# A two-layer recurrent-memory transformer and mixer on one core: weight blocks of one 128-row piece, a ring of their own for the mixer's weights, and one exponential per head group

## The chip, the core and the metric

The kernel runs on one core of a Trainium2 chip. Its engines work side by side and wait for each other through semaphores: TensorE (PE; its weight loads are listed apart as PEld), VectorE (DVE), ScalarE (ACT), GpSimd (POOL) and SyncE (SP). Here SP only issues loads of weights. The metric is the device time of one execution in microseconds (us).

## The reference, cut to what matters

The program is attention layer A, mixer B, A again, B again, each on the layer norm of a residual stream x of 2048 rows by 640 (bfloat16), with the same weights both times.

```python
# A: 64 segments of 32 rows, in order; mem (8 rows) goes from each segment to the next
for s in range(n_seg):
    h = concat([mem, x[32*s:32*s+32]])                     # 40 rows of 640
    q, k, v = h @ Wq, h @ Wk, h @ Wv                       # 32 heads of 192
    scores = where(mask, q @ k.T * scale, -1e9)
    o = (softmax(scores) @ v) @ Wo                         # back to 640
    mem, out[s] = o[:8], o[8:]
# B: token mixing by shifted column groups, then an MLP of 1536
h  = gelu(layernorm(x) @ w1)                               # 640 x 640
x1 = x + concat(four shifted column groups of h) @ w2      # 640 x 640
y  = x1 + gelu(layernorm(x1) @ w3) @ w4                    # 640 x 1536 x 640
```

The weights of A are 31.5 MB, more than the on-chip memory holds beside the activations, and every segment needs all of them.

## The kernel before

Both applications of A run interleaved as two lanes of one loop: step t handles segment t of the first layer and segment t-5 of the second, so that 64 + 5 = 69 steps do all of it. Steps 5 to 63 have both lanes (80 columns), the first five and the last five only one (40 columns). The mixer B runs in 35 chunks of 128 rows (64 of each lane), one for two steps, spread over the attention work of these steps.

A step has 8 groups of 4 heads. `proj` computes k, q (transposed, 6 tiles of 128 rows) and v of a group, and `attend` the scores (`pss`), mask and row minimum on DVE (L569), the exponential on ACT (L577, one instruction per head, each with the row's sum), the normalisation on DVE (L582, L583), the transposes (`pst`, L591), P times V (`pso`, L605) and the output projection into `psy` (L623), which adds up over the step. At the end of a step its first rows go to the next step's input (`hT`, L640): the next step can't begin before.

**Weights.** A's weights are cut into 64 units of 480 KB (half of a group's k, q, v or o; L387-L390). 37 of them stay on the chip (`N_RES`); 27 are loaded anew in each step into a ring of 5 buffers (`wst`, L423-L429). The mixer's weights come in up to 480 KB pieces of three 128-row blocks, through one buffer (`RING_B = 1`, `wstB`, L431-L462): 12 loads of this kind for a chunk, w1 in 2, w2 in 2 (the second in 5 transfers), w3 and w4 in 4 each. All these loads are issued by SP in one order; a load that waits for its buffer holds up those behind it.

**The order** of all instructions on all engines is written out ahead by a planner (`Plan.place`): each operation has an engine, an assumed duration and a due time; the planner places on each engine what can start first, the earlier due first among near ones, with an assumed transfer rate and latency for loads. The hardware then runs each engine's list in that order. A ring buffer or PSUM bank of a class ("P" 3, "S" 2, "B" 2, "y" 1) is handed out by the planner, too.

At the start, POOL copies w1 through on-chip memory into a reordered copy in device memory (`w1d`, L1013-L1026), which the chunks then read.

## Time and profile before

| what | us |
|---|---|
| median of the two runs shown (4161.6 to 4197.4) | 4179.5 |
| the profiled execution | 4201.7 |
| its span, first to last instruction | 4200.0 |
| PE busy / DVE busy / ACT busy in the span | 3679.9 / 2221.0 / 1960.1 |
| end of step 0 (first `hT` copy of L640) | 95.6 |
| end of step 4, start of the two-lane steps | 302.2 |
| end of step 62 (63rd `hT` copy) | 3775.9 |
| end of step 67 (68th `hT` copy) | 4040.8 |
| last attention matmul, then only mixer work | 4096 |

The table gives marks on the time axis; the stretch 302.2 to 3775.9 is 58 steps of both lanes, 59.9 us each. In the rows further down, "releaser" or "<-" names what ended an engine's idle time. The granted clock is TensorE's, as a share of 2.4 GHz (0.5 is 1.2 GHz). DMA share is the mean busy share of the 16 DMA engines; it can pass 1 where packets overlap.

### The profile page before, as it was taken

To read this page: it belongs to the slowest core of one execution; us is meant where nothing else is said; L and a number is where in the kernel's file an instruction comes from. 1 tells how busy PE (TensorE), PEld (TensorE's weight loads), DVE (VectorE), ACT (ScalarE), POOL (GpSimd) and SP (SyncE) were. 2 spreads that over 40 slices of the span, in tenths; PEclk is the share of its full clock that TensorE was granted. 3 is DMA by queue.
4 is the path that set the end of the run, shared out by engine and by line. 5 is a ranking of instruction groups with operands and counts; after the bars stand their busy time and mean duration, and the time that the engine had idled before them with its cause. 6 is when DMAs were issued, how large, how long until landed. Compare 5 with 4: busy or idle time off the path is not lost.

```text
span 4200.0 us, 162257 instructions
## 1 busy us (share of the span) xinstructions
PE 3679.9 (88%) x70351; PEld 3232.6 (77%) x70351; DVE 2221.0 (53%) x6403; ACT 1960.1 (47%) x7380; POOL 280.8 (7%) x489
## 2 busy tenths in 40 slices
PE   6998888889899898989898989888989888989993
PEld 4777877888888787878887888787878777877771
DVE  2455555555555555555555555555545555555452
ACT  2444444444454444544444544444544444445440
POOL 1000000000000000000000000000000000000000
PEclk7999999999999999999999999999999999999995
DMA  9998888888898888988888888888888888889992
GB/s 360 300 312 280 266 267 274 276 281 267 269 289 274 267 277 275 284 273 276 279 271 271 279 273 275 278 263 274 276 254 279 273 275 278 268 280 289 318 298 78
DMA packets 1365962, 1154.32 MB, mean 275 GB/s; under 512 B 44094, under 2 KB 1362380, under 8 KB 1365248
## 3 DMA queue, kind: packets, MB, share of 16 engines
q1 hardware_dynamic: 1357536, 1129.19, 86.0%
q0 software_dynamic: 7712, 14.76, 1.0%
q8 instruction: 552, 9.04, 0.8%
q14 instruction: 162, 1.33, 0.1%
...
## 4 chain that ended last, share of the span: by engine, by line
PE 67%; DMA 25%; issue 2%; SPq 2%; ACT 2%; DVE 1%; POOL 0%; ACTq 0%; POOLq 0%; DVEq 0%
DMA wstB<-in_B_w_dram 19%; PE psv L535 16%; PE psk L503 13%; PE psq L503 12%; PE psy L623 8%; DMA wstB<-w1d 4%; PE psh L928 3%; PE y L948 3%; PE pso L605 3%; PE pss L558 3%; PE pst L591 2%; PE psh L873 1%; PE hs L896 1%; SPq L460 1%; ACT Pm L577 1%
## 5 line engine op out<-in xcount | busy, mean ns | idle before, releaser
L577 ACT ACTIVATE Pm<-pss,sm 80x80 bf16<-80x80 f32 (+1 forms) x2208 | 673.3, 314 | 186.8 <-DVE sm L569 186.2
L540 ACT CAST V<-psv 80x384 bf16<-80x384 f32 (+1 forms) x1104 | 522.1, 474 | 507.4 <-PE psv L535 504.2
L535 PEld LDWEIGHTS <-hT 128*80 128x80 bf16 (+1 forms) x5520 | 586.4, 117 | 213.7 <-issue 15.8
L503 PEld LDWEIGHTS <-wst 128*128 128x128 bf16 x14490 | 611.3, 103 | 24.8 <-issue 5.9
L535 PE MATMUL psv<-wv,hT 128*80 128x384 bf16 (+1 forms) x3105 | 611.5, 332 | 2.3 <-DMA wv<-in_A_Wv_dram 2.1
L611 DVE CAST oT<-pso 128x480 bf16<-128x480 f32 (+1 forms) x552 | 342.3, 620 | 412.9 <-PE pso L605 411.5
L510 ACT CAST qT<-psq 128x480 bf16<-128x480 f32 (+1 forms) x552 | 292.1, 529 | 504.4 <-PE psq L503 493.9
L535 PE MATMUL psv<-wst,hT 128*80 128x384 bf16 (+1 forms) x2415 | 483.6, 332 | 0.7 <-DMA wst<-in_A_Wv_dram 0.4
L503 PE MATMUL psk<-hT,wk 128*128 128x80 bf16 (+1 forms) x9315 | 441.8, 205 | 17.6 <-ACT hT L640 13.0
L623 PE MATMUL psy<-oT,wo 128*128 128x80 bf16 (+1 forms) x10350 | 454.1, 200 | 2.2 <-DVE oT L611 1.5
L503 PE MATMUL psq<-hT,wq 128*128 128x80 bf16 (+1 forms) x9315 | 440.5, 203 | 5.8 <-DMA wq<-in_A_Wq_dram 5.7
L577 ACT ACTIVATION_READ_ACCUMULATOR Pm<-pss,sm 80x1 f32 (+1 forms) x2208 | 437.0, 198 | 0.0
L503 PEld LDWEIGHTS <-wk 128*128 128x128 bf16 x9315 | 396.8, 104 | 40.4 <-issue 22.2
L569 DVE CUSTOM_DVE_ANT_1 pss<-pss,mask 80x320 f32<-80x320 f32 x472 | 232.8, 493 | 358.5 <-PE pss L558 357.8
L623 PEld LDWEIGHTS <-wo 128*128 128x128 bf16 x10350 | 402.1, 100 | 14.7 <-issue 7.9
L596 ACT COPY PT<-pst 80x320 bf16<-80x320 bf16 (+1 forms) x552 | 221.5, 401 | 369.1 <-PE pst L591 365.3
L518 DVE CAST kT<-psk 128x320 bf16<-128x320 f32 (+1 forms) x552 | 256.3, 464 | 246.5 <-PE psk L503 243.6
L503 PEld LDWEIGHTS <-wq 128*128 128x128 bf16 x9315 | 379.0, 102 | 7.2 <-DMA wq<-in_A_Wq_dram 6.7
L503 PE MATMUL psk<-hT,wst 128*128 128x80 bf16 (+1 forms) x7245 | 357.1, 206 | 2.7 <-DMA wst<-in_A_Wk_dram 2.6
L503 PE MATMUL psq<-hT,wst 128*128 128x80 bf16 (+1 forms) x7245 | 342.4, 203 | 4.4 <-DMA wst<-in_A_Wq_dram 4.4
L524 DVE CAST kT<-psk 64x160 bf16<-64x160 f32 (+1 forms) x1104 | 336.7, 305 | 8.3
L623 PE MATMUL psy<-oT,wst 128*128 128x80 bf16 (+1 forms) x6210 | 284.0, 199 | 53.0 <-DVE oT L611 52.0
...
## 6 DMA issues: line engine op xcount, KB each, us to landing
wst<-in_A_Wk_dram SPq DMA_DIRECT2D x483, 480.0 KB, 5.3
wst<-in_A_Wq_dram SPq DMA_DIRECT2D x483, 480.0 KB, 5.5
wst<-in_A_Wv_dram SPq DMA_DIRECT2D x483, 480.0 KB, 5.2
wst<-in_A_Wo_dram SPq DMA_DIRECT2D x414, 480.0 KB, 5.5
wstB<-in_B_w_dram SPq DMA_DIRECT2D x315, 480.0 KB, 4.8
wstB<-w1d SPq DMA_DIRECT2D x35, 480.0 KB, 4.8
...
wstB<-in_B_w_dram SPq DMA_DIRECT2D x35, 160.0 KB, 3.8
```

Source lines behind the costliest of these rows:

```text
L503: nc.tensor.matmul(out=o[:, hf * GCH + cc, 0:N], lhsT=w[:, kc, cc * P:(cc + 1) * P], rhs=h[:, kc, c0:c0 + N], start=(kc == 0), stop=(kc == ...
L510: nc.scalar.copy(out=q[:, :, 0:N], in_=T(pq)[:, :, 0:N])
L518: nc.vector.tensor_copy(out=k4[:, :, 0::3, 0:N], in_=p4[:, :, 0::2, 0:N])
L524: nc.vector.tensor_copy(out=k4[r0:r1, :, j, 0:N], in_=p4[r0:r1, :, 1, 0:N])
L535: nc.tensor.matmul(out=o[0:N, :], lhsT=h[:, kc, c0:c0 + N], rhs=w[:, kc, :], start=(kc == 0), stop=(kc == KC - 1))
L540: nc.scalar.copy(out=v_runs(V_, hf)[0:N], in_=T(pv)[0:N, :].rearrange("n (a b) -> n a b", a=2))
L558: nc.tensor.matmul(out=o[0:N, i * N:(i + w_) * N].rearrange("p (a b) -> p a b", a=w_), lhsT=q[:, c, 0:N], rhs=k_[:, j:j + w_, 0:N], start= ...
L569: nc.vector.tensor_tensor_reduce(out=o, in0=o, in1=maskt[:].unsqueeze(1).to_broadcast([N, HG, N]), scale=-scale, scalar=3.0e38, op0=ALU.ad ...
L577: nc.scalar.activation(out=Pb[0:N, i, 0:N], in_=o[0:N, i * N:(i + 1) * N], func=ACT.Exp, bias=sm_[0:N, 0:1], scale=-1.0, accum_out=sm_[0:N ...
L596: nc.scalar.copy(out=Pt[0:N, :, 0:N], in_=T(pst)[0:N, :, 0:N])
L611: nc.vector.tensor_copy(out=o_[:, :, 0:N], in_=T(pso)[:, :, 0:N])
L623: nc.tensor.matmul(out=o[:, m, c0:c0 + N], lhsT=w[:, cc, m * P:(m + 1) * P], rhs=o_[:, hf * GCH + cc, 0:N], start=st, stop=True, skip_grou ...
```

## The change

Six things, all in the planner's input:

- A's weights are cut into 168 units of one 128-row block of a group: 192 KB for k, q, v (one contraction block, all 768 columns) and 160 KB for o. 102 of them (148,992 bytes a partition, before 142,080) stay; 66 are loaded in each step into a ring of 10 buffers of 192 KB. Over a step this is 12.39 MB instead of 13.27 MB. A projection unit adds its block into all 6 tiles of the group (6 matmuls), where before a unit finished 3 tiles (15 matmuls). The v unit adds into two PSUM banks at once.
- The mixer's weights have a ring of 5 buffers of 160 KB, one 128-row block per load: 34 loads a chunk instead of 12 in 16 transfers. w1, w3 and a rest of w2 are first copied at the start, by POOL's queue, into a reordered copy in device memory (`wbd`), 18 blocks of 160 KB.
- The exponential is one ACT instruction per group, in place in PSUM; the sums are a DVE reduction, and the normalisation reads PSUM.
- The two masked copies of k are two products with a 0/1 column (`halves`) over 128 rows.
- `after=last[0]` makes the projections of the plan follow each other, and o-buffers (`oT`) are 5 instead of 4, v-buffers 2 instead of 3. With them the output projections of the last 4 groups of a step, before 3, are due at its end.
- The planner's assumed rate, latency and look-ahead differ.

The diff, cut to its core:

```diff
-N_RES = 37
-RING_A = 5
-RING_B = 1
+RES_BYTES = 149000
+RING_A = 10
+RING_B = 5
 STEP = 48.0
 PSUM_POOLS = {"y": 1, "P": 3, "S": 2, "B": 2}
-OT_BUFS = 4
-V_BUFS = 3
+OT_BUFS = 5
+V_BUFS = 2
 LAT = 0.2
 PE_LAT = 0.25
-DMA_RATE = 350.0e3
+LOOK = 0.03
+DMA_RATE = 325.0e3
+DMA_LAT = 2.2
 
...
+        for kind in ("k", "q", "v"):
+            ORDER += [(kind, g, kc) for kc in range(KC)]
+        if g:
+            ORDER += [("o", g - 1, c) for c in range(GC)]
+    ORDER += [("o", NG - 1, c) for c in range(GC)]
+    total = sum(2 * w_len(u) for u in ORDER)
+    res_set = set()
+    acc = 0.0
+    share = RES_BYTES / total
+    got = 0
+    for u in ORDER:
+        n = 2 * w_len(u)
+        acc += share * n
+        if acc >= n / 2 and got + n <= RES_BYTES:
+            res_set.add(u)
+            acc -= n
+            got += n
...
         b = Slotted("ra", None)
-        b.make = lambda: wring.tile([P, HSZ], bf16, name="wst", tag=f"ra{b.slot}")
+        b.make = lambda: wring.tile([P, GW], bf16, name="wst", tag=f"ra{b.slot}")
 
         def fn(op):
-            nc.sync.dma_start(out=w_view(T(b), kind), in_=w_src(kind, g, hf))
-        add("SP", 0.06, due, fn, w=(b,), dma=P * HSZ * 2, queue="wa")
-        return b, lambda: w_view(T(b), kind)
-
-    def load_b(nm, a, e, due):
+            nc.sync.dma_start(out=T(b)[:, 0:n], in_=w_src(u))
+        add("SP", 0.06, due, fn, w=(b,), dma=P * n * 2, queue="wa")
...
+        b.make = lambda: wring.tile([P, Dm], bf16, name="wstB", tag=f"rb{b.slot}")
+        k = {"w1": n, "w3": KC + n, "w2": KC + FC}.get(nm)
+        rd = [] if nm == "w4" or (nm == "w2" and n < 4) else [B("wbd", k)]
+            nc.sync.dma_start(out=T(b)[:], in_=src)
...
+    def order_mixer_weights():
+
+        for n in range(KC):
+            def f(op, n=n):
+                o = wbd[n].rearrange("p (kc n) -> p kc n", kc=KC)
+                w1 = B_w1.rearrange("(kc p) n -> p kc n", p=P)
+                if n < 4:
+                    nc.gpsimd.dma_start(out=o, in_=w1[:, :, QD * n:QD * n + P])
+                    return
+                for gi in range(4):
+                    nc.gpsimd.dma_start(out=o[:, :, 32 * gi:32 * gi + 32], in_=w1[:, :, QD * gi + P:QD * gi + QD])
+            add("POOL", 0.9 if n < 4 else 4.0, 20 + n, f, w=(B("wbd", n),), dma=P * Dm * 2)
+
+        def f2(op):
+            for gi in range(4):
+                nc.gpsimd.dma_start(out=wbd[KC + FC][32 * gi:32 * gi + 32, :], in_=B_w2[QD * gi + P:QD * gi + QD, :])
+        add("POOL", 4.0, 26, f2, w=(B("wbd", KC + FC),), dma=P * Dm * 2)
+        for n in range(FC):
+            def f3(op, n=n):
+                o = wbd[KC + n].rearrange("p (kc n) -> p kc n", kc=KC)
+                nc.gpsimd.dma_start(out=o, in_=B_w3.rearrange("(kc p) n -> p kc n", p=P)[:, :, P * n:P * n + P])
+            add("POOL", 0.9, 30 + n, f3, w=(B("wbd", KC + n),), dma=P * Dm * 2)
 
...
             for kind, off in (("k", 0.0), ("q", 0.3 * sl)):
                 pq = ps("P", [P, GC, NS], f32, "ps" + kind)
-                for hf in range(2):
-                    due = s0 + off + hf * 0.1
-                    wb, wv = load_unit(t, (kind, g, hf), due)
-
-                    def fn(op, pq=pq, wv=wv, hf=hf):
+                now = []
+                for kc in range(KC):
+                    due = s0 + off + kc * 0.05
+                    wb, wv = load_unit(t, (kind, g, kc), due)
+
+                    def fn(op, pq=pq, wv=wv, kc=kc):
                         w, o = wv(), T(pq)
-                        for cc in range(GCH):
-                            for kc in range(KC):
-                                nc.tensor.matmul(out=o[:, hf * GCH + cc, 0:N], lhsT=w[:, kc, cc * P:(cc + 1) * P],
-                                                 rhs=h[:, kc, c0:c0 + N], start=(kc == 0), stop=(kc == KC - 1))
-                    add("PE", mm_us(N, k=GCH * KC), due, fn, r=(wb, *hk), a=(pq,))
+                        for c in range(GC):
+                            nc.tensor.matmul(out=o[:, c, 0:N], lhsT=w[:, c * P:(c + 1) * P], rhs=h[:, kc, c0:c0 + N],
+                                             start=pq.begin(), stop=True, skip_group_check=True)
+                    now.append(add("PE", mm_us(N, k=GC), due, fn, r=(wb, *hk), a=(pq,), after=last[0]))
+                last[0] = now
...
-                    for part, (r0, r1, j) in enumerate(((0, 64, 1), (64, P, 2))):
-                        def fk2(op, pq=pq, k_=k_, r0=r0, r1=r1, j=j):
-                            p4 = T(pq)[:].rearrange("p (h c) n -> p h c n", h=2)
-                            k4 = k_[:].rearrange("p (h c) n -> p h c n", h=2)
-                            nc.vector.tensor_copy(out=k4[r0:r1, :, j, 0:N], in_=p4[r0:r1, :, 1, 0:N])
-                        add("DVE", dve_us(2 * N), s0 + off, fk2, r=(pq,), w=(B("kT", G % 2, 1 + part),))
+
+                    def fk2(op, pq=pq, k_=k_):
+                        p4 = T(pq)[:].rearrange("p (h c) n -> p h c n", h=2)
+                        k4 = k_[:].rearrange("p (h c) n -> p h c n", h=2)
+                        for hf in range(2):
+                            nc.vector.tensor_tensor(out=k4[:, hf, 1:3, 0:N],
+                                                    in0=p4[:, hf, 1:2, 0:N].to_broadcast([P, 2, N]),
+                                                    in1=halves[:].unsqueeze(2).to_broadcast([P, 2, N]), op=ALU.mult)
+                    add("DVE", 2 * dve_us(2 * N), s0 + off, fk2, r=(pq,), w=(B("kT", G % 2, 1),))
             V_ = Vt[G % V_BUFS]
+            pv = [ps("P", [NS, GWH], f32, "psv") for _ in range(2)]
+            now = []
+            for kc in range(KC):
+                due = s0 + 0.6 * sl + kc * 0.05
+                wb, wv = load_unit(t, ("v", g, kc), due)
+
+                def fv(op, wv=wv, kc=kc):
+                    w = wv()
+                    for hf in range(2):
+                        nc.tensor.matmul(out=T(pv[hf])[0:N, :], lhsT=h[:, kc, c0:c0 + N],
+                                         rhs=w[:, GWH * hf:GWH * (hf + 1)], start=pv[hf].begin(), stop=True,
+                                         skip_group_check=True)
+                now.append(add("PE", mm_us(GWH, k=2), due, fv, r=(wb, *hk), a=tuple(pv), after=last[0]))
+            last[0] = now
             for hf in range(2):
...
-                o = T(pss)
-                for i in range(HG):
-                    nc.scalar.activation(out=Pb[0:N, i, 0:N], in_=o[0:N, i * N:(i + 1) * N], func=ACT.Exp,
-                                         bias=sm_[0:N, 0:1], scale=-1.0, accum_out=sm_[0:N, 4 + i:5 + i])
-            add("ACT", 4 * 0.31, hi - 4, f2, r=(pss, smk), w=(Pk, B("sm4", G % 4)))
+                o = T(pss)[0:N, 0:HG * N]
+                nc.scalar.activation(out=o, in_=o, func=ACT.Exp, bias=sm_[0:N, 0:1], scale=-1.0)
+            add("ACT", act_us(HG * N) + 0.09, hi - 4, f2, r=(smk,), w=(pss,))
 
             def f3(op):
+                o = T(pss)[0:N, 0:HG * N].rearrange("p (a b) -> p a b", a=HG)
+                nc.vector.reduce_sum(out=sm_[0:N, 4:4 + HG], in_=o, axis=AX.X)
                 nc.vector.reciprocal(out=sm_[0:N, 8:8 + HG], in_=sm_[0:N, 4:4 + HG])
-                nc.vector.tensor_tensor(out=Pb[0:N, :, 0:N], in0=Pb[0:N, :, 0:N],
+                nc.vector.tensor_tensor(out=Pb[0:N, :, 0:N], in0=o,
                                         in1=sm_[0:N, 8:8 + HG].unsqueeze(2).to_broadcast([N, HG, N]), op=ALU.mult)
-            add("DVE", 0.17 + 0.5, hi - 4, f3, r=(B("sm4", G % 4),), w=(Pk,))
+            add("DVE", 0.17 + 2 * dve_us(HG * N), hi - 4, f3, r=(pss,), w=(Pk, smk))
...
-            for hf in range(2):
+            for c in range(GC):
                 due = base + STEP - 1 + 0.02 * g if g >= NG - OT_BUFS + 1 else s0 + 2.0 * sl
-                wb, wv = load_unit(t, ("o", g, hf), s0 + (1.9 if g < NG - 1 else 1.2) * sl + 0.1 * hf)
-
-                def f8(op, wv=wv, hf=hf):
+                wb, wv = load_unit(t, ("o", g, c), s0 + (1.9 if g < NG - 1 else 1.2) * sl + 0.03 * c)
+
+                def f8(op, wv=wv, c=c):
                     w, o = wv(), T(psy)
-                    for cc in range(GCH):
-                        for m in range(KC):
-                            st = first_wo[0]
-                            first_wo[0] = False
-                            nc.tensor.matmul(out=o[:, m, c0:c0 + N], lhsT=w[:, cc, m * P:(m + 1) * P],
-                                             rhs=o_[:, hf * GCH + cc, 0:N], start=st, stop=True, skip_group_check=True)
-                add("PE", mm_us(N, k=GCH * KC), due, f8, r=(wb, B("oT", G % OT_BUFS)), a=(psy,))
+                    for m in range(KC):
+                        nc.tensor.matmul(out=o[:, m, c0:c0 + N], lhsT=w[:, m * P:(m + 1) * P], rhs=o_[:, c, 0:N],
+                                         start=psy.begin(), stop=True, skip_group_check=True)
+                add("PE", mm_us(N, k=KC), due, f8, r=(wb, B("oT", G % OT_BUFS)), a=(psy,))
...
         for i, (a, e) in enumerate(((0, 3), (3, KC))):
-            due = D(0.2 + 0.1 * i)
-            wb, wv = load_b("w1", a, e, due)
             pz = ps("B", [P, 3, XB], f32, "psh")
-
-            def fw(op, a=a, e=e, wv=wv, pz=pz):
-                w, o = wv(), T(pz)
-                for n in range(a, e):
+            for n in range(a, e):
+                due = D(0.15 + 0.04 * n)
+                wb, wv = load_b("w1", n, due)
+
+                def fw(op, n=n, a=a, wv=wv, pz=pz):
+                    w, o = wv(), T(pz)
                     for kc in range(KC):
-                        nc.tensor.matmul(out=o[:, n - a, :], lhsT=w[:, kc, (n - a) * P:(n - a + 1) * P],
+                        nc.tensor.matmul(out=o[:, n - a, :], lhsT=w[:, kc * P:(kc + 1) * P],
                                          rhs=vT[:, kc, 4:XB + 4], start=(kc == 0), stop=(kc == KC - 1))
-            add("PE", mm_us(128, k=KC * (e - a)), due, fw, r=(wb, vTk, B("vTl")), w=(pz,))
+                add("PE", mm_us(128, k=KC), due, fw, r=(wb, vTk, B("vTl")), a=(pz,))
...
-        for kc in range(KC):
-            def f6(op, kc=kc):
-                nc.gpsimd.dma_start(out=xo[:], in_=B_w1[kc * P:(kc + 1) * P, :])
-            add("POOL", 0.9, kc, f6, w=(B("xo"),), dma=P * Dm * 2)
...
+        order_mixer_weights()
```

Three places show how this moves instructions; the rows are of the lists in which the engines run them.

SP, in the middle of the run where a chunk's w4 is loaded (`wstB` from in_B_w_dram); in brackets the semaphores that the load waits for: PE is the release of its buffer, a DMAHW number the landing of an earlier load. Before:

```order
L427 DMA wst<-in_A_Wk_dram 128x5x384 [waits DMAHW6_49,PE_49]
L453 DMA wstB<-in_B_w_dram 128x3x640 [waits DMAHW7_49,PE_49]
L427 DMA wst<-in_A_Wq_dram 128x5x384 [waits DMAHW0_49,PE_49]
L427 DMA wst<-in_A_Wv_dram 128x5x384 [waits DMAHW1_49,PE_49]
L453 DMA wstB<-in_B_w_dram 128x3x640 [waits DMAHW5_49,PE_49]
L427 DMA wst<-in_A_Wo_dram 128x3x640 [waits DMAHW2_49,PE_49]
```

and with the change:

```order
L444 DMA wst<-in_A_Wk_dram 128x768 [waits DMAHW7_49,PE_49]
L444 DMA wst<-in_A_Wk_dram 128x768 [waits DMAHW0_49,PE_49]
L444 DMA wst<-in_A_Wq_dram 128x768 [waits DMAHW1_49,PE_49]
L462 DMA wstB<-in_B_w_dram 128x640 [waits DMAHW2_49,PE_49]
L462 DMA wstB<-in_B_w_dram 128x640 [waits DMAHW3_49,PE_49]
L462 DMA wstB<-in_B_w_dram 128x640 [waits DMAHW4_49,PE_49]
L444 DMA wst<-in_A_Wq_dram 128x768 [waits DMAHW5_49,PE_49]
L462 DMA wstB<-in_B_w_dram 128x640 [waits DMAHW6_49,PE_49]
```

Before, each `wstB` load reuses the one buffer of the load before it, so it stands behind PE's last matmul on that buffer; now the buffer that it reuses is that of five loads before. The DMAHW numbers run from 0 to 7 and begin again: with the change each load waits for the one issued eight loads earlier to land, so that at most eight are under way. In all there are 5846 weight loads on SP, before 2460 transfers.

POOL, at the start. Before, behind the memsets:

```order
L756 DMA xres<-in_A_x_dram 62x640
L761 DMA lnx<-in_A_x_dram 2x640
L767 DMA lnx<-in_A_x_dram 64x640
L862 COPY hTB<-hTB 128x5x8
L1015 DMA xo<-in_B_w_dram 128x640
L677 TENSOR_TENSOR st_146<-st_146,neghalf 128x2
```

and with the change:

```order
L473 DMA wbd<-in_B_w_dram 640x1x128 x4
L476 DMA wbd<-in_B_w_dram 640x1x32 x4
L707 TENSOR_TENSOR st_149<-st_149,neghalf 128x2
L481 DMA wbd<-in_B_w_dram 16x1280 x4
L486 DMA wbd<-in_B_w_dram 640x1x128 x12
L786 DMA xres<-in_A_x_dram 62x640
```

The `st` operation is a part of the first layer norm, which the first projection needs; eight transfers of w1 stand ahead of it now. The first `wstB` load from `wbd` stands 29th on SP's list and waits for the first of these copies.

DVE, one head group with both lanes. Before:

```order
L518 CAST kT_115<-psk 128x2x2x80
L524 CAST kT_115<-psk 64x2x80 x2
L569 ISA pss,sm_130<-pss,mask_78 80x320
L569 ISA sm_130 80x1
L611 CAST oT_125<-pso 128x480
L582 RECIPROCAL sm_130<-sm_130 80x4
L583 TENSOR_TENSOR Pm_120<-Pm_120,sm_130 80x320
```

and with the change:

```order
L545 CAST kT_115<-psk 128x2x2x80
L552 TENSOR_TENSOR kT_115<-psk,halves 128x160 x2
L644 CAST oT_123<-pso 128x480
L602 ISA pss,sm_130<-pss,mask_78 80x320
L602 ISA sm_130 80x1
L614 TENSOR_REDUCE sm_130<-pss 80x4
L615 RECIPROCAL sm_130<-sm_130 80x4
L616 TENSOR_TENSOR Pm_119<-pss,sm_130 80x320
```

One instruction more for DVE in each group (the sums), and the exponentials that ACT does between the mask and the reciprocal are one instead of four. PE's list has as many matmuls and weight loads as before (140,704 rows in both); only their order differs.

## Rows read from the trace of the kernel before

**Rows 1.** Windows (stretch and length; busy us and count per engine; granted clock, DMA share, GB/s).

```profile
0.00:95.60 95.60, 61.54 (x954) 41.58 (x955) 20.11 (x80) 23.75 (x104) 16.95 (x46) 0.72 1.05 364
...
302.20:3775.90 3473.70, 3108.40 (x59073) 2792.75 (x59073) 1918.31 (x5364) 1675.84 (x6205) 225.04 (x374) 0.95 0.88 274
...
3775.90:4040.80 264.90, 239.99 (x5062) 193.77 (x5063) 130.87 (x444) 126.16 (x524) 17.18 (x30) 0.97 0.96 307
...
4096.00:4200.00 104.00, 30.72 (x184) 18.84 (x180) 21.09 (x50) 8.88 (x18) 4.14 (x7) 0.52 0.27 79
```

**Rows 2.** Line L640 from 0 to 3780 us: end-of-step copies, first and last start.

```profile
L640 ACT CAST hT<-psy x63: 192/225/226, 95.6 to 3775.9; 128x80 bf16<-128x80 f32 x58, 128x40 bf16<-128x40 f32 x5
```

**Rows 3.** Waits of PE, 302.2 to 3775.9 us (us in total, times, longest).

```profile
PE y L948 <- DMA wstB<-in_B_w_dram: 87.7, 55, 3.3
PE psh L928 <- DMA wstB<-in_B_w_dram: 66.7, 30, 3.3
PE hs L896 <- DMA wstB<-in_B_w_dram: 56.2, 57, 2.1
PE psy L623 <- DVE oT L611: 46.9, 58, 0.9
PE psh L873 <- DMA wstB<-w1d: 44.6, 29, 2.5
PE pso L605 <- ACT PT L596: 39.3, 58, 0.8
PE pst L591 <- DVE Pm L583: 14.2, 29, 1.0
```

**Rows 4.** Chain of waits, 2078 to 2103 us: start, length, what, matmuls.

```profile
2078.99 0.84 PE psh L928 x15
2079.82 1.07 PE psq L503 x30
...
2081.71 0.15 PE pst L591 x4
2081.87 0.29 PE pss L558 x6
2082.16 0.81 PE psv L535 x5
2082.97 0.29 PE pso L605 x8
...
2086.28 5.95 DMA wstB<-in_B_w_dram
2092.28 1.78 PE psh L928 x15
2094.05 2.00 PE psk L503 x30
...
2101.94 0.83 PE y L948 x6
```

**Rows 5.** Waits of PE in the tail, 4096 to 4200 us.

```profile
PE y L948 <- DMA wstB<-in_B_w_dram: 27.5, 8, 3.7
PE psh L928 <- DMA wstB<-in_B_w_dram: 14.3, 4, 3.8
```

**Rows 6.** Page, part 6: loads, count, size, median us from issue to landing.

```profile
wst<-in_A_Wk_dram SPq DMA_DIRECT2D x483, 480.0 KB, 5.3
...
wstB<-in_B_w_dram SPq DMA_DIRECT2D x35, 160.0 KB, 3.8
```

**Rows 7.** The same in the tail, 4100 to 4200 us, one load at a time.

```profile
wstB<-in_B_w_dram SPq DMA_DIRECT2D x13, 480.0 KB, 3.4
```

**Rows 8.** Timeline of SP, 2030 to 2100 us: start, length of the issue.

```profile
2094.09 0.37 SPq L453 DMA_DIRECT2D wstB<-in_B_w_dram  x1
```

**Rows 9.** Groups of instructions by shape (busy us, mean ns, idle before).

```profile
L577 ACT ACTIVATE Pm<-pss,sm 80x80 bf16<-80x80 f32 x1888 | 584.8, 319 | 144.4 <-DVE sm L569 144.4
...
L569 DVE CUSTOM_DVE_ANT_1 pss<-pss,mask 80x320 f32<-80x320 f32 x472 | 232.8, 493 | 358.5 <-PE pss L558 357.8 <-issue 0.5
```

More of the change, by code (lines that the diff above doesn't have):

```diff
@@ L76, in add @@
         op.i = len(self.ops)
-        preds = set()
+        preds = set(after)
         slots = []
@@ L471, in lanes @@
         return r
+    last = [()]
     def HX(t):
@@ L844, in chunk @@
         psl2 = ps("B", [P, KC, 96], bf16, "psvl")
-        transposes(psl2, vx, 96, D(0.11), (vxk,))
+        transposes(psl2, lnx, 96, D(0.11), (B("lnx", "l"), B("lnx", "x")))
+        if c + 1 < NCH:
+            chunk_loads(c + 1)
         def fe(op):
@@ L885, in chunk, with fw @@
         hs = [ps("B", [XB, HC], f32, "hs") for _ in range(2)]
-        for i, (a, e) in enumerate(((0, 3), (3, 5))):
-            due = D(0.4 + 0.1 * i)
-            wb, wv = load_b("w2", a, e, due)
-            def fw(op, a=a, e=e, wv=wv):
+        for n in range(5):
+            due = D(0.4 + 0.04 * n)
+            wb, wv = load_b("w2", n, due)
+            def fw(op, n=n, wv=wv):
                 w = wv()
-                for n in range(a, e):
-                    off = W2OFF[n] if n < 4 else 0
-                    lhsT = hTB[:, n, off:off + TOK, :].rearrange("p w l -> p (w l)")
-                    for k in range(2):
-                        nc.tensor.matmul(out=T(hs[k])[:], lhsT=lhsT, rhs=w[:, n - a, HC * k:HC * (k + 1)],
-                                         start=(n == 0), stop=(n == 4))
-            add("PE", mm_us(HC, k=2 * (e - a)), due, fw, r=(wb, B("hTB", 0), B("hTB", 1)), a=tuple(hs))
+                off = W2OFF[n] if n < 4 else 0
+                lhsT = hTB[:, n, off:off + TOK, :].rearrange("p w l -> p (w l)")
+                for k in range(2):
+                    nc.tensor.matmul(out=T(hs[k])[:], lhsT=lhsT, rhs=w[:, HC * k:HC * (k + 1)],
+                                     start=hs[k].begin(), stop=True, skip_group_check=True)
+            add("PE", mm_us(HC, k=2), due, fw, r=(wb, B("hTB", 0), B("hTB", 1)), a=tuple(hs))
         for k in range(2):
```

169 lines of the change are left out of this document (63 added, 106 removed).

## The prediction

> **What bounds the kernel now.** I read the windows first, to see where PE is busy and at which clock; then PE's waits, to see what its idle time ends on; then the chain of waits, for the length of PE's pieces of work; then the loads. The 58 two-lane steps run from 302.2 to 3775.9 us [rows 1, 2], so one takes 3473.7/58 = 59.9 us. PE is busy 3108.4/58 = 53.6 us of it and idle 6.3. Of the idle time the four waits for `wstB` make (87.7 + 66.7 + 56.2 + 44.6)/58 = 255.2/58 = 4.4 us [rows 3]; nearly all of the rest is the end of a step, where the last group's scores go through DVE and ACT and PE has nothing else (46.9 + 39.3 + 14.2 = 100.4, 1.7 a step). A's own ring shows next to no wait.
>
> How much work does PE have? From the chain [rows 4], at the full clock: 30 matmuls of k, q or o take 1.07 us, 5 of v 0.81, the scores and P times V of a group 0.29 each, the transposes 0.15. A step has 24 times 30 of the first kind (25.7), 16 times 5 of v (13.0) and 8 groups of the rest (5.8): 44.5 us. A chunk has 85 matmuls like `psh` (0.84 for 15), 34 like `y` (0.83 for 6) and some 30 transposes at the `psh` rate: 4.8 + 4.7 + 1.7 = 11.2, half of it in each step. So 50.1 us of work in a step that takes 59.9. The 3.5 us between 50.1 and the 53.6 busy are partly TensorE's clock: 0.95 granted [rows 1] is a tenth of the time at 1.2 instead of 2.4 GHz, 6.0 us a step. One such place is in the chain: behind a `wstB` wait of 5.95 us, 15 `psh` take 1.78 instead of 0.84 and 30 `psk` 2.00 instead of 1.07, that is 1.9 us lost beside the wait [rows 4].
>
> So the bound in the steady part is PE's work, plus the one buffer of the mixer's ring: its next load can't be issued before PE's last matmul on the block before, and a load needs 3.4 us even alone [rows 7].
>
> **The change, part by part**, against the profiled execution (4201.7 us; the median of the runs shown is 0.5% less).
>
> *The mixer's ring of 5.* The load that PE needs next is issued four blocks ahead. A chunk has 34 blocks over two steps, one in 3.2 us on average, so four blocks are some 12 us, and 160 KB land in 3.8 us beside other loads [rows 6]. The 4.4 us a step go: -255 us. Ends: -255 and, if a fifth stays where blocks stand close together, -204.
>
> *The clock.* With the long waits gone, I expect the full clock in the steps. At most half of 6.0 us can come back, 3.0 a step; at least nothing, if the rest of the 3.5 is something else. I take 2.0, since the one stall in the chain alone lost 1.9 us: -116 us (0 to -174).
>
> *The other ten steps.* In the last one-lane steps PE is idle (264.9 - 240.0)/5 = 5.0 us each [rows 1], 3.1 more than a two-lane step has beside its ring waits (6.3 - 4.4 = 1.9). For ten such steps: -31 us (0 to -31).
>
> *The tail*, mixer alone, 104 us with PE busy for 30.7 [rows 1]. 12 waits for w4 and w3 blocks make 27.5 + 14.3 = 41.8 us [rows 5]. With loads ahead these go, and some waits for the GELU take their place: -35 (-20 to -42).
>
> *The start.* Step 0 needs all of A's weights and moves 364 GB/s [rows 1], so its length is set by loads. Added are 18 blocks of 160 KB, read and written: 5.9 MB, 16 us at that rate: +16. They are small pieces and w1 stands ahead of the first layer norm on POOL and of the 29th load on SP; eight transfers one behind the other at 3.8 us would be 30 us (0 to +30).
>
> *Traffic.* 12.39 + 2.79 MB a step instead of 13.27 + 2.79. The 284 GB/s that a step of 59.9 - 6.4 = 53.5 us would need is under the 307 of the one-lane steps [rows 1]. No gain is taken, the cover being PE's 50 us; without it a step's loads take 15.18 MB at 364 GB/s, 42 us. All this holds if small transfers move as fast: 480 KB ones gave 364 GB/s in step 0 with several under way [rows 1]. The Trainium skill (DMA: Bandwidth & Descriptors, Bandwidth) speaks against cutting them: it asks for transfers of 1 MiB or more for three quarters of the peak. By it the result would be that of rival 2, 4540, and by the rows it is 3760; the step 0 row shows that the rule doesn't bind at 480 KB, and no row shows 192 KB.
>
> *SP.* 66 + 17 = 83 issues a step at 0.37 us [rows 8] are 31 us of in-order work; 0.65 us each would make SP the bound.
>
> *Attention.* Four exponentials of 319 ns become one over 320 columns, at something like the 493 ns of the mask pass over the same data; the sum is another such pass on DVE [rows 9]. The end-of-step chain shortens by 1.28 - 0.49 and grows by 0.49: about 0.3 us less. DVE goes from 33.1 to some 37 us of a step: it stays off the path. v now takes both its PSUM banks at once, and the third belongs to q, so k must be out of its bank before v begins; q's 1.07 us and pieces between cover that in most groups. I take 0; ends -17 (0.3 a step) and +58 (1 us a step).
>
> *Finer projection units and more deferred o work.* As many matmuls, and a unit of 5 or 6 costs PE what a third of 15 does: `psy` already adds round-robin into its five tiles at 1.07 for 30. 0; if the extra o group fills half of the 1.7 us at a step's end, -50.
>
> Sum: 4201.7 - 255 - 116 - 31 - 35 + 16 = 3781; on the scale of the median, 0.5% less, 3760 us. All good ends together give 4201.7 - 255 - 174 - 31 - 42 - 17 - 50 = 3633, or 3613; all bad ones 4201.7 - 204 - 20 + 30 + 58 = 4066, or 4044. Half of the bad side is likely enough: 3620 to 3930 is the forecast's own range.
>
> **The rivals.**
>
> 1. *Eight loads in flight.* SP's list makes each load wait for the one eight earlier. Eight of 480 KB were plenty; now 83 loads a step, eight at a time, need 10.4 times the landing time. At 3.8 us [rows 6] that is 39 us and hidden. If a small load landed as late as a 480 KB one, 5.3 us, it would be 55.0 us: 58 x 4.9 = 284 saved instead of 371, 3868, or 3850. Against it: 160 KB landed in 3.8 in the same traffic.
>
> 2. *The same, on the slow side.* The landing time passes 5.8 us (59.9/10.4), from where a step is longer than now. At 6.2, that is 5.3 and half of the 1.9 by which load raises it over the 3.4 of a lone one [rows 6, 7], a step takes 64.5: 58 x 4.6 = +267, in the ten others some 11 us each, with tail and start 4560, or 4540. For it: more than twice as many transfers, with their completions, for the same bytes. Against it: rows 6. The rule above is of this kind; its chance is this rival's.
>
> 3. *The stall re-forms.* SP's list is in order, and a `wst` load that waits for PE holds the `wstB` loads behind it. If PE's list has mixer blocks just behind their loads, the 4.4 us stay, and with them the clock's loss; only the tail gains: 4201.7 - 35 + 16 = 4183, or 4160, no change. If half of both stays, it is 3997, or 3975.
>
> 4. *All bad ends of the terms together*: 4044, still faster.
>
> **How the numbers follow.** Forecast 0.73; better than 3620 0.07; between 3930 and 4096 (rival 3 with half, rival 4, rival 1 with landing somewhat over 5.3) 0.12; no change (rival 3 in full) 0.04; slower (rival 2) 0.04. Rival 1 at 3850 lies within the forecast's range, with 0.08 of its 0.73. A change of 2% is what a measurement of this kernel can tell, 4096 and 4263 us. Faster by over 2%: 0.73 + 0.07 + 0.12 = 0.92. The range of 8 in 10 is 3600 to 3940.
>
> **What would show it.** In the profile after: waits of PE for `wstB` under 1 us a step; granted clock 0.98 or more between the first and last steps; two-lane steps of 53 to 54 us with PE busy for 50 to 52; a tail of some 65 us; landing of `wst` near 4 us and PE's waits for it still near nothing; ACT busy down by a third or more, DVE up by a tenth. The forecast is wrong if PE waits for `wst` in mid-step (rival 1 or 2), if `wstB` waits stay (rival 3), or if the gaps at a step's end grow by more than 1 us.

## The result, and the profile after

The changed kernel takes **3825.1 us** (median; 3813.2 to 3836.9) against 4179.5: ratio **0.9152**, 95% interval 0.8944 to 0.936, so 8.5% faster. A second measurement of it, beside other kernels, gave 3814.2 us and 0.916 [0.9125, 0.9196]. Forecast were 3760 us, in a range from 3600 to 3940: the kernel got faster as forecast, and the time lies in the range, 1.7% above the forecast. The profiled execution took 3813.2 us; it is compared with the 4201.7 us of the one before.

The windows of the changed kernel, with the columns of [rows 1] (stretch and length; busy us of PE, PE's weight loads, DVE, ACT, POOL; granted clock, DMA share, GB/s): step 0, the four one-lane steps behind it, the 58 two-lane steps, steps 63 to 67 (63 still has both lanes, the others one), and the last step with the tail.

```profile
0.00:111.80 111.80, 74.50 (x954) 46.82 (x955) 21.41 (x90) 17.25 (x48) 25.79 (x50) 0.66 0.99 328
111.80:311.80 200.00, 188.12 (x4045) 144.64 (x4044) 105.96 (x389) 73.97 (x201) 12.09 (x21) 0.97 0.93 296
311.80:3445.40 3133.60, 2992.11 (x59067) 2668.23 (x59068) 2079.75 (x5825) 1276.72 (x2954) 207.57 (x374) 1.00 0.91 287
3445.40:3703.90 258.50, 243.59 (x5057) 191.39 (x5055) 140.95 (x485) 93.35 (x245) 16.36 (x30) 0.98 0.94 299
3703.90:3811.50 107.60, 76.63 (x1232) 55.52 (x1231) 54.55 (x168) 28.69 (x71) 9.44 (x18) 0.80 0.66 202
```

The bounds of the steps come from the end-of-step copies, the line that answers [rows 2]; it moved from L640 to L670.

```profile
L670 ACT CAST hT<-psy x68: 174/226/227, 111.8 to 3703.9; 128x80 bf16<-128x80 f32 x58, 128x40 bf16<-128x40 f32 x10
```

A two-lane step went from 59.9 to 3133.6/58 = 54.03 us. PE's busy time in these steps fell from 3108.4 [rows 1] to 2992.1 us for the same number of matmuls, at a granted clock of 1.00 instead of 0.95; its idle time fell from 365.3 to 141.5 us. What the idle time ends on, in the same stretch (us in total, times, longest), beside [rows 3]:

```profile
PE psv L566 <- ACT qT L537: 26.4, 86, 0.5
PE pso L638 <- ACT PT L629: 22.9, 57, 0.5
PE psy L653 <- DMA wst<-in_A_Wo_dram: 22.9, 30, 1.9
PE psy L653 <- DVE oT L644: 21.7, 29, 0.8
PE psk L529 <- DMA wst<-in_A_Wk_dram: 11.7, 25, 1.3
PE psq L529 <- DMA wst<-in_A_Wq_dram: 9.7, 20, 1.6
...
PE psv L566 <- DVE kT L552: 8.9, 28, 0.3
PE psv L566 <- DMA wst<-in_A_Wv_dram: 1.9, 5, 0.5
PE pst L624 <- DVE Pm L616: 0.8, 2, 0.6
...
PE y L975 <- DMA wstB<-in_B_w_dram: 0.5, 2, 0.3
PE hs L925 <- DMA wstB<-wbd: 0.4, 1, 0.4
```

Three things are to be seen. The four waits for `wstB`, 255.2 us before, are 0.9. The waits at a step's end (on `oT`, `PT`, `Pm`) fell from 100.4 to 45.4. And two kinds are new: A's streamed units (`wst`) cost 22.9 + 11.7 + 9.7 + 1.9 = 46.2 us, and v's banks, held by q (`qT`) and k (`kT`), 35.3 us.

The waits of the tail, from 3755 us on, beside [rows 5]: weights make 1.5 us, and VectorE's part of the GELU (`h2T`, `hTB`) now stands where they were.

```profile
PE y L975 <- DVE h2T L747: 4.2, 3, 2.5
PE psh L957 <- DVE h2T L747: 3.1, 2, 2.2
PE hs L925 <- DVE hTB L747: 2.9, 2, 1.8
PE y L975 <- DMA wstB<-in_B_w_dram: 1.5, 4, 0.7
```

The loads, as in [rows 6] (count, size, median us from issue to landing): a unit of 192 KB lands in 4.2 us, where 480 KB took 5.3.

```profile
wst<-in_A_Wk_dram SPq DMA_DIRECT2D x1104, 192.0 KB, 4.2
```

In step 0, where the loads set the time, the stretch from 30 to 90 us moved 377 GB/s before and 327 after (the first row is of the kernel before):

```profile
30.00:90.00 60.00, 43.11 (x635) 28.64 (x636) 11.25 (x46) 15.11 (x70) 3.42 (x7) 0.61 1.08 377
30.00:90.00 60.00, 45.70 (x572) 28.24 (x571) 9.87 (x40) 8.23 (x22) 0.00 (x0) 0.56 0.99 327
```

The exp and the sum, as in [rows 9] (busy us, mean ns of one, idle before): one exp of 494 ns stands for four of 319, and the sum takes VectorE 485 ns.

```profile
L609 ACT ACTIVATE pss<-pss,sm 80x320 f32<-80x320 f32 x472 | 233.4, 494 | 424.3 <-DVE sm L602 424.1
...
L614 DVE TENSOR_REDUCE sm<-pss 80x4 f32<-80x320 f32 x472 | 229.1, 485 | 188.2 <-ACT pss L609 186.5
```

### The profile page after: what moved, and what is told of

Its sections match the earlier page's. It is cut to its first block, busy times and chain, and to the rows that moved or that the text cites. A ratio compares the mean times of both kernels' runs of the same rounds, so it can differ in the third digit from the quotient of the medians.

```text
span 3811.5 us, 164549 instructions
## 1 busy us (share of the span) xinstructions
PE 3574.9 (94%) x70351; PEld 3106.6 (82%) x70351; DVE 2402.6 (63%) x6957; ACT 1490.0 (39%) x3516; POOL 271.2 (7%) x493
## 4 chain that ended last, share of the span: by engine, by line
PE 74%; DMA 18%; DVE 3%; ACT 2%; issue 1%; POOL 0%; SPq 0%; POOLq 0%; DVEq 0%; ACTq 0%
PE psv L566 20%; PE psy L653 13%; PE psk L529 12%; PE psq L529 12%; DMA wst<-in_A_Wk_dram 6%; DMA wst<-in_A_Wq_dram 5%; DMA wst<-in_A_Wo_dram 4%; PE pso L638 4%; PE pss L591 3%; PE y L975 3%; PE psh L957 2%; PE pst L624 2%; DMA wst<-in_A_Wv_dram 2%; ACT qT L537 1%; PE psh L903 1%
## 5 line engine op out<-in xcount | busy, mean ns | idle before, releaser
L566 PE MATMUL psv<-wv,hT 128*80 128x384 bf16 (+1 forms) x3312 | 799.1, 331 | 38.4 <-ACT qT L537 26.8
L529 PEld LDWEIGHTS <-wst 128*128 128x128 bf16 x13248 | 609.2, 100 | 76.2 <-DMA wst<-in_A_Wk_dram 32.7
L653 PE MATMUL psy<-oT,wo 128*128 128x80 bf16 (+1 forms) x10350 | 590.0, 199 | 30.5 <-DVE oT L644 25.5
L529 PE MATMUL psq<-hT,wq 128*128 128x80 bf16 (+1 forms) x9936 | 569.9, 199 | 6.0 <-DMA wq<-in_A_Wq_dram 4.7
L529 PE MATMUL psk<-hT,wk 128*128 128x80 bf16 (+1 forms) x9936 | 535.3, 199 | 15.9 <-ACT hT L670 11.9
L653 PEld LDWEIGHTS <-wo 128*128 128x128 bf16 x10350 | 466.8, 99 | 69.5 <-issue 45.4
L609 ACT ACTIVATE pss<-pss,sm 80x320 f32<-80x320 f32 (+1 forms) x552 | 261.7, 474 | 516.7 <-DVE sm L602 516.1
L653 PE MATMUL psy<-oT,wst 128*128 128x80 bf16 (+1 forms) x6210 | 417.1, 199 | 28.7 <-DMA wst<-in_A_Wo_dram 27.5
L529 PE MATMUL psq<-hT,wst 128*128 128x80 bf16 (+1 forms) x6624 | 412.4, 199 | 16.5 <-DMA wst<-in_A_Wq_dram 14.1
L614 DVE TENSOR_REDUCE sm<-pss 80x4 f32<-80x320 f32 (+1 forms) x552 | 254.3, 461 | 210.8 <-ACT pss L609 207.9
L653 PEld LDWEIGHTS <-wst 128*128 128x128 bf16 x6210 | 296.4, 99 | 44.5 <-DMA wst<-in_A_Wo_dram 34.7
```

The source lines that it names most:

```text
L529: nc.tensor.matmul(out=o[:, c, 0:N], lhsT=w[:, c * P:(c + 1) * P], rhs=h[:, kc, c0:c0 + N], start=pq.begin(), stop=True, skip_group_check= ...
L566: nc.tensor.matmul(out=T(pv[hf])[0:N, :], lhsT=h[:, kc, c0:c0 + N], rhs=w[:, GWH * hf:GWH * (hf + 1)], start=pv[hf].begin(), stop=True, sk ...
L609: nc.scalar.activation(out=o, in_=o, func=ACT.Exp, bias=sm_[0:N, 0:1], scale=-1.0)
L614: nc.vector.reduce_sum(out=sm_[0:N, 4:4 + HG], in_=o, axis=AX.X)
L653: nc.tensor.matmul(out=o[:, m, c0:c0 + N], lhsT=w[:, m * P:(m + 1) * P], rhs=o_[:, c, 0:N], start=psy.begin(), stop=True, skip_group_check ...
```

## The experiments

The theory was that the number of mixer loads that may be ahead of PE, and the clock that comes back with the stall, are the whole gain; the rivals were that other parts (finer units, less traffic, the single exp, the planner's constants) carry some of it. Each ratio is to the kernel before, measured on the same chip. One thing limits all but one of them: an edit that the planner sees deals a new order of the work, so what an experiment measures is its edit and that new order together. Where it decides the reading, it is said.

**1. The changed kernel with one mixer slot.**

```
-RING_B = 5
+RING_B = 1
```

> The changed kernel with one buffer in the mixer's ring instead of 5. Ring theory (the gain is that PE no longer waits for the next mixer block): each of a chunk's 34 blocks must then be loaded behind PE's last matmul on the block before: 4.1 us landing, 0.3 issue, 0.3 us of matmuls, 4.7 us, 160 us a chunk where two steps take 108. So the ring would bound the kernel: some 35 x 160 = 5600 us, PE's wait for wstB over 20 us a step. Rival, traffic (the gain is the smaller and better cut traffic of A's weights) or attention (one exponential): little changes, under 3950 us.

Measured: 5270.5 us, ratio 1.2645 [1.2583, 1.2706]. PE's waits in its two-lane steps:

```profile
PE y L975 <- DMA wstB<-in_B_w_dram: 661.4, 332, 3.6
PE psh L957 <- DMA wstB<-wbd: 115.6, 147, 2.4
```

With three smaller ones (40.4 and 4.9 on `hs`, 40.1 on the other `psh`) they make 862 us, and the clock of the whole run falls to 0.854. That is 14.9 us a step, where the expectation has over 20 and some 5600 us: the size was overrated, the cause holds. Every other part of the change is in this kernel, and it is 26% slower than the kernel before: the slots carry the gain. It waits 590 times, where the kernel before with its one slot of 480 KB waits 171 times [rows 3]: over three times as often, with smaller loads and more of them.

**2. The kernel before with two mixer slots, and nothing else.** A slot of 480 KB more, one kept unit less.

```
-N_RES = 37
+N_RES = 36
-RING_B = 1
+RING_B = 2
```

> The kernel before with two mixer buffers of 480 KB instead of one; for the room 36 instead of 37 of A's units stay on the chip, 28 instead of 27 are loaded a step (13.76 instead of 13.27 MB). Everything else as before: 480 KB units, four exponentials, old order of projections. Ring theory: with the next block under way while PE works on one, most of the 4.4 us of wstB waits a step and the half clock behind them go: 3830 to 3920 us. Traffic theory: 3% more bytes and no gain, 4180 to 4300. Attention theory: no gain, about 4180.

Measured: 3811.6 us, ratio 0.9144 [0.9109, 0.918], the ratio of the whole change, and better than the range of the ring theory. Its two-lane steps (windows as above), and what PE's idle time in them ends on:

```profile
301.60:3425.70 3124.10, 2998.63 (x59073) 2698.03 (x59074) 1912.74 (x5363) 1673.64 (x6204) 241.00 (x374) 0.99 0.98 314
```

```profile
PE psy L623 <- DVE oT L611: 43.4, 58, 0.8
...
PE psq L503 <- DMA wst<-in_A_Wq_dram: 18.3, 27, 2.4
...
PE pst L591 <- DVE Pm L583: 12.8, 29, 0.4
```

No wait for `wstB` is left, PE is busy for 2998.6 us against 2992.1 after the change, and the step takes 53.86 us against 54.03, although this kernel moves 314 GB/s and the changed one 287. So one more slot gives the whole gain, and all the other parts together net nothing, each kernel with the order that it was dealt.

**3. Three mixer slots of 160 KB**, the memory of the one slot before.

```
-RING_B = 5
+RING_B = 3
```

> The changed kernel with three mixer slots of 160 KB: the same 480 KB that the kernel before gave its one slot, cut in three. If what counts is that the next load is out while a unit is used, three are nearly enough: 3810 to 3870. Rival, what counts is how many bytes lie ahead, and 480 KB are as short as before: TensorE waits again for wstB by 100 to 255 us in the two-lane steps, 3950 to 4150.

Measured: 3946.0 us, ratio 0.9492 [0.9457, 0.9526], between the two expectations and just under the rival's, whose waits it has.

```profile
PE y L975 <- DMA wstB<-in_B_w_dram: 49.6, 62, 2.6
PE psh L903 <- DMA wstB<-wbd: 48.3, 37, 2.3
PE psh L957 <- DMA wstB<-wbd: 36.6, 60, 2.3
```

The same 480 KB, cut in three, leave 134.5 us of the 255.2; five slots (800 KB) leave 0.9, and two of 480 KB (960 KB) none. As far as kernels with different units and orders can be compared, both count: a load must be out while another block is in use, and what is out must last PE through the stretch in which its blocks stand close together.

**4. The changed kernel with the four exps back.** On ScalarE four exps with their sums, on VectorE no sum.

```
-  nc.scalar.activation(out=o, in_=o, func=ACT.Exp, bias=..., scale=-1.0)
+  for i in range(HG):
+      nc.scalar.activation(out=Pb[0:N, i, 0:N], in_=o[0:N, i*N:(i+1)*N], func=ACT.Exp, ..., accum_out=...)
...
-  nc.vector.reduce_sum(out=sm_[0:N, 4:4 + HG], in_=o, axis=AX.X)
```

> The changed kernel with the four exponentials and their sums on ACT as before, and the normalisation from the on-chip copy. ACT gets some 12 us a step more, DVE 4 us less. Ring theory: both lie beside PE's work, within 1% of the changed kernel, 3790 to 3870 us. Attention theory: it loses a good part of the gain, over 3950.

Measured: 3892.5 us, ratio 0.9339 [0.9309, 0.9368], 78 us more than the changed kernel's 3814.2 and between the two expectations. Its two-lane steps:

```profile
317.20:3520.10 3202.90, 3045.84 (x59068) 2707.78 (x59069) 1852.51 (x5363) 1629.62 (x6204) 249.18 (x374) 0.98 0.88 281
```

Of 69 us more, 15.6 are idle time (157.1 against 141.5) and 53.7 are busy time of the same matmuls: the clock. Where it falls, PE's timeline of this kernel shows, at the end of a two-lane step (start, length, what, and in brackets the idle time before it):

```profile
590.23 0.32 PE L624 MATMUL pst<-ident,Pm 80*80 80x80 bf16 x4 [0.90 <-DVE Pm L616]
591.11 0.45 PE L638 MATMUL pso<-PT,V 80*128 80x80 bf16 x8 [0.56 <-ACT PT L629]
592.30 0.82 PE L653 MATMUL psy<-oT,wo 128*128 128x80 bf16 x10 [0.75 <-DVE oT L644]
592.93 0.54 PE L653 MATMUL psy<-oT,wst 128*128 128x80 bf16 x5
```

and the windows of that place show the clock, 1.00 before, 0.85 and then 0.58:

```profile
590.20:593.20 3.00, 1.66 (x27) 1.49 (x28) 0.66 (x1) 0.42 (x1) 0.00 (x0) 0.85 0.61 216
593.20:596.20 3.00, 2.69 (x48) 2.56 (x47) 0.58 (x2) 0.23 (x1) 0.00 (x0) 0.58 0.27 76
```

The changed kernel at the end of the same step:

```profile
579.80:582.80 3.00, 1.74 (x45) 1.54 (x42) 0.66 (x1) 0.42 (x1) 0.00 (x0) 1.00 0.88 276
582.80:585.80 3.00, 2.69 (x75) 2.58 (x72) 1.54 (x5) 0.23 (x1) 0.00 (x0) 1.00 0.54 178
```

There PE waits only 0.51 (`PT`), 0.75 (`oT`) and 0.31 us (`hT`), and the clock stays. The wait of 0.90 on `Pm` ahead of them is what the longer chain of four exps adds; five `psy` matmuls take 0.54 instead of 0.34 us behind it. In the 58 two-lane steps the granted clock falls to its lower level 26 times, in the changed kernel 3 times. But the order of the work is new here too, and experiments 6 to 8 show that this matters.

**5. The changed kernel with the planner's old constants.**

```
-LOOK = 0.03 / DMA_RATE = 325.0e3 / DMA_LAT = 2.2
+LOOK = 0.12 / DMA_RATE = 350.0e3 / DMA_LAT = 1.6
```

> The changed kernel with the planner's numbers of before (look-ahead 0.12, rate 350, latency 1.6). If the order that these numbers give matters, PE's waits for wst rise from 0.8 us a step to 2 or more, 3900 or more; the ring theory alone says 3800 to 3880, since the buffers are the same.

Measured: 3798.0 us, ratio 0.9116 [0.908, 0.9152], within the error of the new ones, and the waits for `wst` do not rise (47.6 us in the two-lane steps against 46.2). The constants bring nothing that can be told.

**6. The kernel before with the single exp**, one mixer slot still (the exp and the sum as in the changed kernel).

> The kernel before with the single exp and the sum on VectorE, and nothing else of the change: one mixer slot still. If the exps' price is the chain at the end of a step (four exps cost the changed kernel 69 us in its two-lane steps, 54 of them at the lower clock), the same chain is shorter here and the time falls by 40 to 90 us: 4080 to 4130. Rival: the time of the kernel before is set by the single mixer slot, whose loads start when the slot is given back, so what the chain saves is handed to the next mixer wait: 4150 to 4190, no change.

Measured: 4126.3 us, ratio 0.9902 [0.9867, 0.9937]. It gains 1%, and no more: waits for `wstB` of 190.5 us stay in its two-lane steps. The time lies in the range of the first theory, but not by its cause. The waits at a step's end are what they were (47.0 + 36.0 + 15.2 = 98.2 us, 100.4 before); it is the waits for `wstB` that fell, by 65 us. Whether the exp or the new order did that is open.

**7. Two mixer slots and the single exp.** Experiment 2 with the exp and the sum of the changed kernel, and the planner's durations for them.

> The kernel before with two mixer slots (36 kept units) and the single exp. In the two-slot kernel with four exps, TensorE waited 12.8 us on Pm, 16.4 us on PT and the clock fell 17 times in 58 two-lane steps. If the exps' price is that chain, most of both goes: 3740 to 3790. Rival, the four exps are hidden in this order of work and only the changed kernel's own order laid them open: 3800 to 3830, the time of two slots with four exps (3811.6).

Measured: 3917.1 us, ratio 0.9405 [0.9368, 0.9442]: both theories missed, it is slower than with four exps. Its waits in the two-lane steps:

```profile
PE psq L503 <- DMA wst<-in_A_Wq_dram: 34.4, 39, 2.2
PE y L948 <- DMA wstB<-in_B_w_dram: 29.0, 24, 2.5
PE psv L535 <- DMA wst<-in_A_Wv_dram: 21.8, 38, 1.5
```

Waits for loads are back, 29.0 us on `wstB` and 65.8 on `wst`, at the same bytes. Place by place, 42,786 of TensorE's 140,704 rows differ from experiment 2, and most of SyncE's: the planner dealt another order, loads included.

**8. The same with the order of experiment 2.** The exp is the single one, the planner is told the durations of the four.

```
-add("ACT", act_us(HG * N) + 0.09, hi - 4, f2, r=(smk,), w=(pss,))
+add("ACT", 4 * 0.31, hi - 4, f2, r=(smk,), w=(pss, B("sm4", G % 4)))
...
-add("DVE", 0.17 + 2 * dve_us(HG * N), hi - 4, f3, r=(pss,), w=(Pk, smk))
+add("DVE", 0.17 + 0.5, hi - 4, f3, r=(pss, B("sm4", G % 4)), w=(Pk, smk))
```

> Two mixer slots and the single exp again, but the planner is told the durations of the four exps, so that TensorE's and SyncE's instructions stand in the order of the two-slot kernel with four exps (3811.6 us); with its own durations the single exp moved 42,786 of TensorE's 140,704 rows and the time was 3917.1. If the loss was that new order, it is gone and the shorter chain at the step's end shows: 3770 to 3815. Rival, the single exp itself costs time in this kernel (the sum on VectorE, one score tile held longer): 3880 to 3930.

Measured: 3774.1 us, ratio **0.9087** [0.9045, 0.9129]. This is the one pair in which TensorE's and SyncE's order is the same in every row: against 0.9144 [0.9109, 0.918] the single exp gains some 0.6%, and the intervals overlap. In the profiled two-lane steps it is 3117.4 us against 3124.1:

```profile
303.30:3420.70 3117.40, 2989.99 (x59073) 2685.44 (x59074) 2116.31 (x5827) 1298.86 (x2956) 200.97 (x374) 1.00 0.98 314
```

```profile
PE psq L503 <- DMA wst<-in_A_Wq_dram: 22.3, 39, 1.6
...
PE psv L535 <- DMA wst<-in_A_Wv_dram: 15.2, 28, 1.9
```

The waits on `Pm`, 12.8 us in experiment 2, are gone, but those for `wst` rose from 26.3 to 41.3 us, and PE's idle time is no shorter (127.4 us against 125.5). What the single exp gains here is busy time, 2990.0 us against 2998.6: the clock falls 8 times in these steps instead of 17.

So the 3.2% between experiments 7 and 8 (0.9405 against 0.9087), the same instructions in another order, are the order's. By the same token the 78 us of experiment 4 can't be put down to the exps alone.

**9. v's two banks one after the other.** Each of v's two PSUM banks is filled from all blocks before the next is begun; the units are held through both. (The waits named in the expectation are those above: 35.3 and 46.2 us.)

```
+units = [load_unit(t, ("v", g, kc), s0 + 0.6 * sl + kc * 0.05) for kc in range(KC)]
+for hf in range(2):
+    for kc in range(KC):
+        ... one matmul into pv[hf] from units[kc], a=(pv[hf],)
```

> The changed kernel with the two PSUM banks of v filled one after the other instead of side by side per 128-row block. Theory: the 35.3 us that v waited for the copies of qT and kT in the 58 two-lane steps come from asking for two free banks at once; one at a time they go, and the time falls to 3775 to 3800. Rival: the six units of v are held through both halves, so the ring of ten gives its slots back later and the waits on streamed units (46 us in those steps) grow by as much or more: 3825 to 3900.

Measured: 3792.0 us, ratio 0.9104 [0.9062, 0.9146].

```profile
PE psv L565 <- DMA wst<-in_A_Wv_dram: 33.1, 56, 2.0
PE psy L653 <- DVE oT L644: 21.7, 29, 0.8
PE psk L529 <- DMA wst<-in_A_Wk_dram: 21.6, 39, 1.4
PE psq L529 <- DMA wst<-in_A_Wq_dram: 17.4, 34, 1.5
```

Both happened: the waits on `qT` and `kT` went from 35.3 to 0.3 us, and those on streamed units from 46.2 to 77.8 (with 5.7 on Wo). The waits on `PT` went too. The net is 22 us, within the error of either.

**10. The same with fourteen slots for streamed units**, and 0.88 MB more streamed per step (two units of v and three of o; the 0.78 MB of the expectation are the bytes asked for, which whole units do not meet).

```
-RES_BYTES = 149000 / RING_A = 10
+RES_BYTES = 142900 / RING_A = 14
```

> The changed kernel with v's banks filled one after the other (3792.0 us) and fourteen slots instead of ten for streamed units, paid for with 6,100 bytes per partition of kept units, so 0.78 MB more streamed per step. If the 78 us of waits on streamed units in the two-lane steps are waits for a slot, they fall to 20 to 40: 3735 to 3775. Rival, they are the transfers themselves, which more bytes make longer: 3795 to 3850.

Measured: 3839.0 us, ratio 0.9222 [0.9176, 0.9267].

```profile
PE y L975 <- DMA wstB<-in_B_w_dram: 50.7, 57, 2.2
PE psv L565 <- DMA wst<-in_A_Wv_dram: 34.3, 44, 2.0
```

The waits on `wst` fell a little, from 77.8 to 61.4 us, and waits for `wstB` of 52.6 came, at 303 GB/s instead of 291: the rival's time, by way of the mixer's loads, which stand in the same queue.

**11. The same with eight slots**, and 0.23 MB less streamed per step (two units of v less, one of o more; the expectation's 0.38 MB are again the bytes asked for).

```
-RES_BYTES = 149000 / RING_A = 10
+RES_BYTES = 152000 / RING_A = 8
```

> The changed kernel with v's banks filled one after the other (3792.0 us), eight slots instead of ten for streamed units, and 3,000 more bytes per partition of kept units, so 0.38 MB less streamed per step. Fourteen slots with 0.78 MB more streamed took 3839.0. If the bytes set the waits on streamed units, the slope of that run (47 us for 0.78 MB) gives 23 us back: 3760 to 3780. Rival, the slots set them (six of the eight are held while v's two banks are filled): 3800 to 3860.

Measured: 4083.4 us, ratio 0.9775 [0.973, 0.9819], far past the rival.

```profile
332.00:3695.60 3363.60, 3068.20 (x59064) 2716.45 (x59065) 2063.40 (x5828) 1289.81 (x2956) 223.24 (x374) 0.98 0.85 264
```

Against experiment 9 (3096.3 us, of them 2979.9 busy) PE is idle for 179 us more in the two-lane steps and busy for 88 more. Waits on `wst` are 175.2 us, and those at a step's end 102.4, where experiment 9 has 21.7 on `oT`. Two slots less, with the order that they bring, cost most of what the whole change gains; four more, in experiment 10, took off 16 us of waits. The reason that the expectation gives is wrong: v has five units in a group, not six, and only 14 of its 40 in a step are streamed here (966 loads in 69 steps), so it holds two slots, not six. Slots, bytes and order changed together in both runs; what makes eight so much worse than ten, and how much of the 47 us of experiment 10 is bytes, stays open.

## Why the prediction was right, and where it missed

In the profiled executions the forecast was 4201.7 - 421 = 3781 us, and 3813.2 was measured. Term by term:

| stretch | forecast | measured |
|---|---|---|
| step 0 | +16 | +16.2 (95.6 to 111.8) |
| the other steps (1 to 4 and 63 to 67) | -31 | -13.0 |
| two-lane steps | -255 - 116 = -371 | -340.1 |
| last step and tail | -35 | -51.6 (159.2 to 107.6) |

The stall from which the clock's term was taken, in PE's timeline of the kernel before (in brackets the idle time):

```profile
2092.28 1.78 PE L928 MATMUL psh<-vT,wstB 128*128 128x128 bf16 x15 [2.53 <-DMA wstB<-in_B_w_dram]
```

- **The ring: right.** Waits for `wstB` went from 255.2 to 0.9 us, and experiment 2 shows that the second slot alone does it. The third rival (the stall re-forms) fell with it.
- **The clock: right to the microsecond, by luck.** Busy time fell by 3108.4 - 2992.1 = 116.3 us, where 116 was one stall of 2.0 us in each step, taken from one place in the chain [rows 4]. That place was misread: 5.95 us is the load from issue to landing, and PE waited 2.53 us for it, behind waits of 0.79 and 0.87. Nor is it one a step: the clock falls 73 times in the 58 steps before and 3 times after, so that a fall cost 116.3/70 = 1.7 us on average. The bounds were 0 and 174; what was sound is that the gain lay in short stretches at the lower level behind a stall, which experiment 4 shows from the other side.
- **Step 0: right by luck.** The +16 was 5.9 MB more at an unchanged 364 GB/s. By the windows it moved 364 x 95.6 = 34.8 MB before and 328 x 111.8 = 36.7 MB after: 1.9 MB more, some 5 us, and the other 11 us are the lower rate. Whether the size of the loads, the eight in flight or SP's issues set that rate is not shown.
- **The two-lane steps: 31 us too good.** The step that failed is that A's own ring, which had next to no wait before, was left at that and v's two banks at 0. Measured are 46.2 us on `wst` and 35.3 on the banks, which the text had bounded (up to 1 us a step) and then dropped, since q's matmuls were to cover k's copy "in most groups"; the wait is on q's own bank, 26.4 of the 35.3. Against these 81.5 stand 55.0 us less at a step's end, which the prediction had as a bound only (-17 and -50). Its own sign of being wrong, waits for `wst` in mid-step, came at 0.8 us a step.
- **Why `wst` waits at all.** The prediction compared GB/s with a mean (284 against 307) and found room. A mean says nothing of the single load: that of k that PE waits for at 2079 us took 5.46 us to land, where the median is 4.2. Ten slots of 192 KB are 1920 KB, where five of 480 KB were 2400. Experiment 11 suggests that the ring stands near an edge, 175 us of waits with eight slots, though the order changed with it. The cause of these waits stays open.
- **The other steps: less than half.** There are nine, not ten. In the last five, 15.5 us of `wstB` waits went and 7.2 of `wst` waits came.
- **The tail: mis-sized.** The window of [rows 5] began at 4096 us, while the last projections' copy stood at 4040.8. From there on, waits for `wstB` were 27.5 + 14.8 + 9.3 + 4.6 = 56.2 us, and 1.5 now; 10.2 us of GELU waits took their place, as foreseen. Experiment 2, with depth alone, has a tail of 119.4 us (-39.8).
- **Attention: right at a fixed order** (experiment 8: -6.7 us in the two-lane steps, forecast 0, ends -17 and +58), though what it saved was busy time at the lower clock and not the wait at a step's end. Of the marks named, ACT's busy time fell by 24% (1960 to 1490 us) and not by a third.
- **Traffic and small loads: right in the steps, not in step 0.** Landing was 4.2 us, so eight loads in flight and 10.4 rounds a step give 10.4 x 4.2 = 44 us, under the 54 of a step: rivals 1 and 2 did not come. But where the loads set the time, the small ones moved less: 327 GB/s against 377, from 30 to 90 us of step 0. The Trainium skill (DMA: Bandwidth & Descriptors, Bandwidth) asks for 1 MiB or more per transfer and gives 341 GB/s for one of 1 MB. This trace agrees in the direction, but overlapping loads of 160 and 192 KB come near the skill's figure, with 327 GB/s, and those of 480 KB pass it, with 377. Where bytes grew in the steps, the time grew (experiment 10, at 303 GB/s), with slots and order changed beside them.
- **All the rest nets nothing,** as far as kernels with orders of their own can be compared: an order alone was worth 3.2% in experiments 7 and 8. Experiment 2 has the whole gain with 9% more bytes in its loads (1162.6 MB against 1069.2), coarse units, four exps and the old planner. What the other parts gain at a step's end they give back in step 0 (+16), on `wst` and on v's banks.

The best kernel was experiment 8, 3774.1 us: the kernel before with a second mixer slot and the single exp. Its interval overlaps that of experiment 2; against the changed kernel's 0.916 [0.9125, 0.9196] it is ahead by 0.8%, with intervals that barely overlap.
